# Attention scores of five units as one product per window for both heads, issued two units ahead, without filler products

## Chip, cores and metric

The kernel runs on one core of a Trainium2 chip. The metric is device time of one execution in microseconds; the median of three runs of the kernel before is 808.26 us (806.73 to 808.89).

## What is computed

Windowed attention with eight memory keys per head, then a dense mixture of four experts, then a two-layer network. Cut to what matters:

```python
for c in range(nc):                          # chunks of 32 queries
    k_full = concat(mem_k, k[16 before .. 8 after the chunk])   # 64 keys
    scores = scale * q_c @ k_full.T
    a = exp(scores - max); a = a / (sum(a) + 1e-9)
    out[chunk] = a @ v_full
x = out as (1536 tokens, 512)
x = sum over e of p[:, e] * (relu(x @ w1[e]) @ w2[e])           # 4 experts, 1024 wide
h = x @ w_in
return (max(h, 0) + alpha * min(h, 0)) @ w_out                  # 2048 wide
```

## The kernel before

A **unit** is 128 tokens with all eight heads, four pairs z of two heads e; there are 12 (`NU`), taken in the order of `TURN`. Within a unit four windows of 32 queries see 64 keys each. A unit goes through stages, written as a generator (`unit`): scores on PE into the two PSUM banks of `two`, maximum and subtraction on DVE (`mx`, `pe`), the exponential on ACT (`pe`), four transposes on PE (`t`), a copy on ACT (`pt`), the product with the values on PE (`x`; the 65th column of the values gives the sum), the sums on ACT (`dn`), their reciprocal and the scaling on DVE (`rd`, `xs`), transposes back on PE (`xt`), and the sums, differences and splits into high and low parts (`acc`, `st`, `xh`, `xl`) that the Strassen products of the first layer read. `pe`, `pt` and `xs` are one buffer each, used by all units in turn. Below, scores(2) or x(2) is that stage of the third unit, counted from 0.

Each engine runs its instructions in the order written (`Pinned`). While the first tile of the dense layers has no input, `att_cycle` sets that order: one call starts unit m (scores, maximum, subtraction), then issues x(m-1), exp(m), filler products (`keep_warm`), the transposes of m and those back of m-1. The fillers are products of a zeroed part of `xh` with itself whose result nobody reads: 10 after scores(0), 5 after each of units 1 to 5; from unit 6 on `SOON` puts the first dense products (`a`) there, and `FILL` five more fillers before t(7) and t(8). Once `att["five"]` is 3 the calls end, and the remaining units are woven between the dense products by a planner's clock (`att_poll`).

Scores of a unit are 32 products of 64 rows (the head's dimension), 32 columns and 64 keys, two heads side by side on rows 0 to 63 and 64 to 127. The two ring buffers of `qk` hold two units, `RING_V` half units of values. SP issues all loads in the order written: `load_qk(u + 2)` after scores(u), halves of the values after the x that frees a buffer; the weights of the first layer (`raw`) are four transfers of 128 KB, tied by `begun` to the number of units started.

The dense layers fill the rest of the run: expert layers, conversion of the last weights, the last network.

Of the kernel before, what the change touches and what calls it, by code (L numbers as in the profile page):

```python
# [10 lines left out]
F32 = mybir.dt.float32  # L11
F32R = mybir.dt.float32r
# [38 lines left out]
class Pinned:  # L51


    def __init__(self, tc, eng):
        self.tc, self.eng = tc, eng
# [7 lines left out]
        return call  # L63


@with_exitstack
def tile_kernel(ctx: ExitStack, tc: tile.TileContext, qk, v, wa, wq, dpt, alpha, out):
    nc = tc.nc
    scale = 1.0 / float(D) ** 0.5
    pe_, dve, act, pool, sync = (Pinned(tc, e) for e in (nc.tensor, nc.vector, nc.scalar, nc.gpsimd, nc.sync))  # L70

    cp = ctx.enter_context(tc.tile_pool(name="cp", bufs=1))
    xp = ctx.enter_context(tc.tile_pool(name="xp", bufs=1))
    bp = ctx.enter_context(tc.tile_pool(name="bp", bufs=1))
# [4 lines left out]
    two = scores.enter_context(tc.tile_pool(name="sc", bufs=1, space=bass.MemoryType.PSUM)).tile(  # L79
        [P, 2, 512], F32, tag="two", name="two")  # L80
# [24 lines left out]
    tiny = cp.tile([P, PAD], F32, name="tiny")  # L105
# [9 lines left out]
    now = [0.0]  # L115
# [35 lines left out]


    xh = xp.tile([P, 14, NCOL], F32R, name="xh")
    xl = xp.tile([P, 14, NCOL], F32R, name="xl")

    half = NCOL // 2
    acc = xp.tile([P, KD, 2, 2, half], F32, name="acc")
    acc_all = acc.rearrange("p o t a n -> p o (t a n)")

# [83 lines left out]
    def mm(*a, n, took=None, **kw):  # L243
        pe_.matmul(*a, **kw)
        now[0] += took or 0.013 + n / 2.4e3


    qk_all = bp.tile([P, RING, QW + KW], F32, tag="gg", bufs=2, name="qk")
    qk_t = [qk_all[:, i] for i in range(RING)]
    v_t = [bp.tile([P, V_ROOM], F32, name=f"v{i}", **tag)[:, :VW].rearrange("p (e z w d) -> p e z w d", e=2, z=HP, w=NW)  # L250
           for i, tag in enumerate((dict(tag="w2", bufs=4), dict(tag="w2", bufs=4), dict(tag="fr"), *2 * [dict(tag="v", bufs=2)]))]
    for vt in v_t:
        for e in range(2):
            (pool, dve)[e].memset(vt[:, e], 0.0)
# [5 lines left out]
    def v_of(hu):  # L260
        return v_t[hu % RING_V]

    def load_qk(u, half=slice(0, 2)):
        if u >= NU:
            return
        i = 2 * u % RING
        sync.dma_start(qk_all[:, i + half.start:i + half.stop].rearrange("p h x -> p (h x)"),
                       qk[TURN[u], :, half].rearrange("p h x -> p (h x)"))

    v_next = [0]  # L270

    def load_v(hu):
        assert hu == v_next[0]
        v_next[0] += 1
        if hu >= 2 * NU:
            return
        for e in range(2):
            sync.dma_start(v_of(hu)[e::2, e].rearrange("p z w d -> p (z w d)"), v[TURN[hu // 2], e, :, hu % 2])

    def unit(u):  # L280

# [1 line left out]
        cols = slice(c * BLK, (c + 1) * BLK)  # L283
        win = [slice(w * WIN, (w + 1) * WIN) for w in range(NW)]

        s_ps = two[:, :, :2 * HP * KEYS].rearrange("p e (z k) -> p e z k", k=KEYS)
        now[0] += T_SW
        for half in range(2):
# [9 lines left out]
        load_qk(u + RING // 2)  # L298
        for hu in FIRST_V[u + 1] if u + 1 < len(FIRST_V) else ():
            load_v(hu)  # L300
        mx = cp.tile([P, 2, 2 * HP], F32, tag="mx", bufs=2, name=f"mx{u}")
        dve.tensor_reduce(out=mx, in_=s_ps, axis=AX.X, op=ALU.max)
        dve.tensor_tensor(
            out=pe.rearrange("p z k e -> p e z k"), in0=s_ps,
            in1=mx.unsqueeze(3).to_broadcast([P, 2, 2 * HP, KEYS]), op=ALU.subtract,
        )
        yield LATE
        act.activation(pe, pe, AF.Exp, scale=scale)
        yield LAT[0]
        t_ps = bank(f"t{u}")  # L310
# [11 lines left out]
        for z in range(2 * HP):  # L322
            half, i = divmod(z, HP)
            if z in CUT:
                n = CUT[z]
                parts.append((z, n, bank(f"x{u}_{z}")[:, :2 * n * (D + 1)].rearrange("p (z e d) -> p z e d", e=2, d=D + 1)))
            z0, _, x_ps = parts[-1]
            for w in range(NW):
                mm(x_ps[win[w], z - z0], pt[:, z, win[w]], v_of(2 * u + half)[:, :, i, w], n=2 * (D + 1), took=T_X,
                   start=True, stop=True)  # L330
            if i == HP - 1:
                load_v(2 * u + half + RING_V)
# [65 lines left out]
    def att_poll(force=False):  # L398

        while True:  # L400
            due = [x for x in att["live"] if x[0] <= now[0] and clear(x[2])]
            room = att["next"] < NU and len(att["live"]) < LIVE and clear(att["next"])
            if due:
                x = due[0]
                try:
                    att["stage"][x[2]] += 1
                    lat = next(x[1])
                    x[0] = now[0] + lat
                except StopIteration:
                    att["live"].remove(x)  # L410
                    att["over"].add(x[2])
                    while att["done"] in att["over"]:
                        att["done"] += 1
            elif room and att["start"] <= now[0]:
                g = unit(att["next"])
                att["start"] = now[0] + (PACE0 if force else PACE)
                att["next"] += 1
                x = [0.0, g, att["next"] - 1]
                att["live"].append(x)
                x[0] = next(g) + now[0]  # L420
                att["stage"][x[2]] = 1
            elif force:
                times = [x[0] for x in att["live"] if clear(x[2])]
                if room:
                    times.append(att["start"])
                now[0] = max(now[0], min(times))
                continue
            else:
                return
            if force:  # L430
                return

    def att_cycle():

        m, t0 = att["next"], now[0]
# [23 lines left out]
        x = live[m] = [now[0], unit(m), m]  # L459
        att["live"].append(x)  # L460
        att["next"] += 1
        advance(x)
# [16 lines left out]
    part = {}  # L479
# [626 lines left out]
LATE = 1.6  # L1106
# [100 lines left out]
```

## Time and profile before

| | us |
|---|---|
| median of three runs | 808.26 |
| the profiled execution, its own time | 807.49 |
| span in its trace | 805.7 |
| PE busy | 795.4 (99%) |
| DVE, ACT, POOL busy | 577.4, 324.9, 573.1 |
| PE's share of the chain that ended last | 92% |

The profiled execution is 0.77 us below the median. A timeline row gives start, length, engine, operation, written tile <- read tiles, count, and in brackets the idle time before it with what ended it. Two rows of one engine may overlap by about 0.1 us, since the next starts while the last one drains. A product in float32 appears as two records.

### The profile page before, as it was taken

To read this page: it belongs to the slowest core of one execution; us is meant where nothing else is said; L and a number is where in the kernel's file an instruction comes from. 1 tells how busy PE (TensorE), PEld (TensorE's weight loads), DVE (VectorE), ACT (ScalarE), POOL (GpSimd) and SP (SyncE) were. 2 spreads that over 40 slices of the span, in tenths; PEclk is the share of its full clock that TensorE was granted. 3 is DMA by queue.
4 is the path that set the end of the run, shared out by engine and by line. 5 is a ranking of instruction groups with operands and counts; after the bars stand their busy time and mean duration, and the time that the engine had idled before them with its cause. 6 is when DMAs were issued, how large, how long until landed. Compare 5 with 4: busy or idle time off the path is not lost.

```text
span 805.7 us, 13680 instructions
## 1 busy us (share of the span) xinstructions
PE 795.4 (99%) x5127; PEld 722.9 (90%) x5127; DVE 577.4 (72%) x1009; ACT 324.9 (40%) x726; POOL 573.1 (71%) x598
## 2 busy tenths in 40 slices
PE   9899999999999999999999999999999999999997
PEld 7689989989989989889889899999899988998996
DVE  4676367687687777777777778589975777676554
ACT  4667423224224134133133133145452664565441
POOL 3786768687797696696696793297764878978621
PEclk9999999999999999999999999999999999999999
DMA  8981121231331341321332312001002122221004
GB/s 255 312 281 32 53 67 52 104 132 40 118 105 40 118 144 40 118 93 51 118 119 66 118 39 92 1 27 53 27 26 92 59 73 92 79 92 67 1 1 156
DMA packets 29730, 71.62 MB, mean 89 GB/s; under 512 B 4448, under 2 KB 10592, under 8 KB 29664
## 3 DMA queue, kind: packets, MB, share of 16 engines
q1 hardware_dynamic: 29664, 70.75, 26.3%
q8 instruction: 40, 0.66, 0.3%
q14 instruction: 26, 0.21, 0.1%
HBM read 59.18 MB, written 11.56 MB: 88 GB/s over the span
## 4 chain that ended last, share of the span: by engine, by line
PE 92%; POOL 2%; DVE 2%; DMA 1%; ACT 1%; issue 1%; SPq 0%; DVEq 0%; POOLq 0%; ACTq 0%
PE y L61 48%; PE d L61 12%; PE c L61 12%; PE a L61 12%; PE b L61 6%; DMA qk<-in_qk 1%; PE two L61 1%; POOL gg L61 1%; PE x L61 1%; POOL xl L61 1%; POOL wl L61 1%; PE t L61 1%; PE wps0.0_88 L61 0%; DVE pe L61 0%; DVE mx L61 0%
## 5 line engine op out<-in xcount | busy, mean ns | idle before, releaser
L61 POOL TENSOR_TENSOR gg<-g,gg 128x384 fp32r<-128x384 f32 x192 | 207.2, 1091 | 111.7 <-ACT gg L61 111.1
L61 PE MATMUL y<-gg,wh 128*128 128x512 f32 (+1 forms) x816 | 244.6, 377 | 0.3 <-POOL gg L61 0.3
L61 DVE TENSOR_TENSOR acc<-y,acc 128x512 f32<-128x512 f32 (+1 forms) x244 | 162.5, 677 | 69.7 <-PE y L61 69.6
L61 PEld LDWEIGHTS y<-gg,wh 128*128 128x128 f32 x816 | 151.8, 188 | 24.8 <-POOL gg L61 0.6
L61 PE MATMUL y<-gg,wl 128*128 128x512 f32 (+1 forms) x408 | 153.8, 377 | 0.0
L61 ACT CAST gg<-g 128x384 fp32r<-128x384 f32 x192 | 95.9, 512 | 122.1 <-DVE g L61 120.4
L61 POOL TENSOR_TENSOR wl<-raw,wh 128x256 fp32r<-128x256 f32 (+1 forms) x110 | 112.1, 1024 | 29.4 <-ACT wh L61 27.4
L61 PE MATMUL y<-wh,gg 128*128 128x512 f32 x384 | 120.6, 390 | 0.0
L61 POOL TENSOR_TENSOR wl<-s,wh 128x256 fp32r<-128x256 f32 x88 | 67.2, 767 | 33.4 <-ACT wh L61 33.2
L61 PEld LDWEIGHTS y<-gg,wl 128*128 128x128 f32 x408 | 76.6, 188 | 12.1 <-issue 0.2
L61 PEld LDWEIGHTS y<-wh,gg 128*128 128x128 f32 x384 | 72.1, 188 | 14.7
L61 ACT COPY u<-a 128x384 f32<-128x384 f32 x48 | 23.1, 481 | 151.3 <-PE a L61 150.2
L61 PE MATMUL y<-wl,gg 128*128 128x512 f32 x192 | 74.9, 390 | 0.0
L61 PE MATMUL a<-xh,wh 128*128 128x384 f32 x184 | 62.0, 337 | 0.0
L61 PE MATMUL a<-xh,wl 128*128 128x384 f32 x184 | 61.8, 336 | 0.0
L61 PE MATMUL d<-xh,wh 128*128 128x384 f32 x184 | 61.8, 336 | 0.0
L61 PE MATMUL a<-xl,wh 128*128 128x384 f32 x184 | 61.6, 335 | 0.0
L61 PE MATMUL d<-xh,wl 128*128 128x384 f32 x184 | 61.6, 335 | 0.0
L61 PE MATMUL d<-xl,wh 128*128 128x384 f32 x184 | 61.6, 335 | 0.0
L61 DVE TENSOR_TENSOR u<-b,u 128x384 f32<-128x384 f32 x48 | 26.7, 556 | 48.2 <-PE b L61 47.9
L61 PE MATMUL c<-xl,wh 128*128 128x384 f32 x176 | 58.9, 335 | 0.0
L61 PE MATMUL c<-xh,wh 128*128 128x384 f32 x176 | 58.8, 334 | 0.0
(129 smaller groups left out, 1562.0 us busy)
## 6 DMA issues: line engine op xcount, KB each, us to landing
fr<-in_wq SPq DMA_DIRECT2D x32, 512.0 KB, 3.9
raw<-in_wa SPq DMA_DIRECT2D x28, 512.0 KB, 3.8
w2s<-fl SPq DMA_DIRECT2D x32, 256.0 KB, 2.4
raw<-w2s SPq DMA_DIRECT2D x16, 512.0 KB, 3.5
qk<-in_qk SPq DMA_DIRECT2D x11, 624.0 KB, 5.6
v<-in_v SPq DMA_DIRECT2D x48, 130.0 KB, 4.8
out<-acc SPq DMA_DIRECT2D x12, 256.0 KB, 2.4
pb<-p_dram SPq DMA_DIRECT2D x6, 384.0 KB, 3.7
```

What stands on the lines that cost most here:

```text
L61: return self.tc.keep_in_program_order(f(*a, **kw))
```

## The change

For units 1 to 5 (`WIDE_U` = 6) the keys of a pair of heads stand in a block diagonal: the rows of one head hold its keys, the other half is zero (`clear_k`). One product of 128 rows, 32 columns and 128 keys then gives the scores of both heads: 16 products a unit for 32. Such a unit's scores use one bank of `two`, units in turn (`u % 2`). `att_cycle` for these units issues scores(m+2) in call m, after x(m), and `keep_warm` is called for unit 0 alone. The subtraction moves from the scores' stage to the exponential's. The values of units 1, 2, 4 and 5 come in whole units (`WHOLE`), into `both_v` and a part of `acc` that is not yet written; q and keys of these units are two inputs of their own (`qa`, `ka`), in three slots. `xl` becomes two halves, of which the second first holds the block-diagonal keys. The tables `NEXT_QK`, `FIRST_V`, `NEXT_V` say which loads follow which unit. The bytes loaded for a unit stay 624 KB and 520 KB.

```diff
+    xl = Halves(half, lambda t: xp.tile([P, 14, half], F32R, tag=f"xl{t}", name=f"xl{t}"))
+    both_k = xp.tile([P, 14 * half], F32, tag="xl1", name="both_k")
+    both_v = bp.tile([P, 2, 4, NW * (D + 1)], F32, tag="gg", bufs=2, name="both_v")
...
+    def clear_k(u, engines):
+        for e in range(2):
+            engines[e].memset(wide_k(u)[e * D:(e + 1) * D, 1 - e], 0.0)
...
+        if both(u):
+            sync.dma_start(wide_q(u), qa[u - 1])
+            for e in range(2):
+                sync.dma_start(wide_k(u)[e * D:(e + 1) * D, e], ka[u - 1, e * D:(e + 1) * D])
+            return
...
+            s_ps = two[:, u % 2].rearrange("p (z e k) -> p e z k", e=2, k=KEYS)
...
+        for z in range(2 * HP if both(u) else 0):
+            for w in range(NW):
+                mm(s_ps[win[w], :, z], qv[:, z, win[w]], kv[:, z // HP, z % HP, :, w * STEP:w * STEP + KEYS],
+                   n=2 * KEYS, took=T_X, start=True, stop=True)
+        for half in range(0 if both(u) else 2):
...
         dve.tensor_reduce(out=mx, in_=s_ps, axis=AX.X, op=ALU.max)
+        if both(u):
+            yield LATE
         dve.tensor_tensor(
...
-        yield LATE
+        if not both(u):
+            yield LATE
...
+        att["turn"] += 1
+        if m < WIDE_U:
+            if m == 0:
+                begin_unit(0)
+                at(0, 1)
+                keep_warm(0)
+            at(m, 2)
+            if m == 0:
+                begin_unit(1)
+            at(m + 1, 1)
+            at(m - 1, 4)
+            rest()
+            if m < WIDE_U - 1:
+                at(m, 3)
+            if m + 2 < WIDE_U:
+                begin_unit(m + 2)
...
+WIDE_U = 6
+WHOLE = {1: 0, 2: 1, 4: 0, 5: 1}
+NEXT_QK = {0: (3,), 1: (4,), 2: (5,), 3: (6,), 5: (7,)}
+FIRST_V = {0: ((2, None),), 1: ((3, 0), (3, 1))}
+NEXT_V = {1: ((4, None),), 2: ((5, None),), 3: ((6, 0), (6, 1)), 4: ((7, 0), (7, 1)), 5: ((8, 0),)}
```

PE at the end of the wide units, in the order of the kernel before, from the last of x(4) (the digit in a name is the unit; `two` are scores, here of unit 6):

```order
L61 MATMUL x4_3_628<-v4_118,pt_129 32x130 x4
L61 MATMUL keep5_651<-xh_109 128x384 x5
L61 MATMUL t5_657<-ident_76,pe_131 128x128 x4
L61 MATMUL xt4_663<-ident_76,xs_130 128x128 x4
L61 MATMUL two_75<-qk_113 32x64 x32
L61 MATMUL x5_0_712<-v0_114,pt_129 32x130 x8
L61 MATMUL x5_0_712<-v1_115,pt_129 32x130 x4
L61 MATMUL x5_3_727<-v1_115,pt_129 32x130 x4
```

And of the change, from t(4):

```order
L61 MATMUL t4_507<-ident_76,pe_142 128x128 x4
L61 MATMUL xt3_515<-ident_76,xs_141 128x128 x4
L61 MATMUL x4_0_526<-both_v_111,pt_140 32x130 x12
L61 MATMUL x4_3_539<-both_v_111,pt_140 32x130 x4
L61 MATMUL t5_562<-ident_76,pe_142 128x128 x4
L61 MATMUL xt4_568<-ident_76,xs_141 128x128 x4
L61 MATMUL two_75<-qk_112 32x64 x32
L61 MATMUL x5_0_625<-acc_113,pt_140 32x130 x12
L61 MATMUL x5_3_638<-acc_113,pt_140 32x130 x4
```

The fillers (`keep5`) that stood ahead of t(5) are gone, and scores(5), which stood behind t(4), now stand ahead of it, so that PE has no scores between x(4) and xt(4).

ACT in the same place before, from the copy of t(4) (`pe <- pe` is the exponential, here of unit 5):

```order
L61 COPY pt_129<-t4_561 128x512
L61 COPY acc_111<-xt3_567 128x4x128
L61 CAST xh_109<-st2_474 128x4x128
L61 CAST xh_109<-acc_111 128x4x128
L61 ACTIVATE dn4_635<-x4_0_613,tiny_83 128x6
L61 ACTIVATE dn4_635<-x4_3_628,tiny_83 128x2
L61 ACTIVATE pe_131<-pe_131 128x512
```

And of the change:

```order
L61 COPY pt_140<-t4_507 128x512
L61 ACTIVATE pe_142<-pe_142 128x512
L61 COPY acc_113<-xt3_515 128x4x128
L61 CAST xh_109<-st2_444 128x4x128
L61 CAST xh_109<-acc_113 128x4x128
L61 ACTIVATE dn4_548<-x4_0_526,tiny_83 128x6
L61 ACTIVATE dn4_548<-x4_3_539,tiny_83 128x2
```

The exponential of unit 5 moves from behind the sums of unit 4 (`dn4`) to ahead of them, and with it the copy of xt(3) and two casts stand between the two.

SP before, from its first transfer to the first weights of the dense layers (`raw0`):

```order
L61 DMA qk_113<-in_qk 128x624 x2
L61 DMA qk_113<-in_qk 128x1248
L61 DMA v0_114<-in_v 64x520 x2
L61 DMA v1_115<-in_v 64x520 x2
L61 DMA qk_113<-in_qk 128x1248
L61 DMA v2_116<-in_v 64x520 x2
L61 DMA v3_117<-in_v 64x520 x2
L61 DMA raw0_0_181<-in_wa 128x256 x2
```

And of the change, from the second half of the values of unit 0, which has the same two q-and-key loads ahead of it (`in_qa`, `in_ka` are queries and keys; `both_v` and `acc` take the values of units 1 and 2):

```order
L61 DMA v1_115<-in_v 64x520 x2
L61 DMA qk_112<-in_qa 128x512
L61 DMA both_k_110<-in_ka 64x736 x2
L61 DMA both_v_111<-in_v 64x1040 x2
L61 DMA qk_112<-in_qa 128x512
L61 DMA both_k_110<-in_ka 64x736 x2
L61 DMA acc_113<-in_v 64x4x260 x2
L61 DMA both_k_110<-in_qa 128x512
L61 DMA both_k_110<-in_ka 64x736 x2
L61 DMA v2_116<-in_v 64x520 x2
L61 DMA v3_117<-in_v 64x520 x2
L61 DMA raw0_0_243<-in_wa 128x256 x2
```

The two weight transfers move from behind q and keys of three units and values of two to behind q and keys of five units and values of four. On ACT the two casts that read them stand where they stood, ahead of the sums of unit 2.

## Rows read from the trace of the kernel before

**Rows 1.** The profile's page: busy time of each engine, and TensorE's granted clock.

```profile
PE 795.4 (99%) x5127; PEld 722.9 (90%) x5127; DVE 577.4 (72%) x1009; ACT 324.9 (40%) x726; POOL 573.1 (71%) x598
...
PEclk9999999999999999999999999999999999999999
```

**Rows 2.** Busy time by stretch: us, then busy us per engine, clock, DMA share, GB/s.

```profile
8.40:47.10 38.70, 35.50 (x889) 28.64 (x889) 22.90 (x54) 25.75 (x63) 22.60 (x29) 1.00 0.93 296
47.10:70.00 22.90, 22.09 (x414) 19.51 (x414) 15.31 (x37) 15.95 (x39) 18.57 (x18) 1.00 0.59 188
70.00:805.70 735.70, 730.60 (x3735) 669.35 (x3733) 535.13 (x910) 281.12 (x623) 527.61 (x540) 1.00 0.22 73
```

**Rows 3.** PE in order of time: start us, us, what, idle before it and its releaser.

```profile
13.06 1.07 PE L61 MATMUL two<-qk 64*32 64x64 f32 x64
14.07 1.09 PE L61 MATMUL x<-v,pt 128*32 128x130 f32 x32
15.09 1.16 PE L61 MATMUL keep<-xh 128*128 128x384 f32 x5
16.49 0.66 PE L61 MATMUL t<-ident,pe 128*128 128x128 f32 x4 [0.24 <-ACT pe L61]
16.98 0.60 PE L61 MATMUL xt<-ident,xs 128*128 128x128 f32 x4
17.51 0.96 PE L61 MATMUL two<-qk 64*32 64x64 f32 x64
18.40 1.09 PE L61 MATMUL x<-v,pt 128*32 128x130 f32 x32
...
22.36 0.74 PE L61 MATMUL two<-qk 64*32 64x64 f32 x51 [0.48 <-DMA qk<-in_qk]
...
23.95 1.09 PE L61 MATMUL x<-v,pt 128*32 128x130 f32 x32
...
32.24 0.86 PE L61 MATMUL x<-v,pt 128*32 128x130 f32 x21
```

**Rows 4.** DVE in order of time, one lap of the attention stage.

```profile
14.28 0.69 DVE L61 TENSOR_REDUCE mx<-two 128x8 f32<-128x512 f32 x1 [1.99 <-PE two L61]
15.08 0.69 DVE L61 TENSOR_TENSOR pe<-two,mx 128x512 f32<-128x512 f32 x1
15.69 0.19 DVE L61 RECIPROCAL rd<-dn 128x8 f32<-128x8 f32 x1
15.98 0.76 DVE L61 TENSOR_TENSOR xs<-x,rd 128x384 f32<-128x384 f32 x2
```

**Rows 5.** ACT in order of time, the same lap and the next casts.

```profile
15.01 0.48 ACT L61 ACTIVATE dn<-x,tiny 128x6 f32<-128x6 f32 x2 [1.14 <-PE x L61]
15.80 0.63 ACT L61 ACTIVATE pe<-pe 128x512 f32<-128x512 f32 x1 [0.31 <-DVE pe L61]
16.34 0.60 ACT L61 CAST xh<-acc 128x512 fp32r<-128x512 f32 x1
...
17.66 0.59 ACT L61 COPY acc<-xt 128x512 f32<-128x512 f32 x1
18.14 0.72 ACT L61 CAST wh<-raw 128x256 fp32r<-128x256 f32 x2
```

**Rows 6.** DMA issues from 9 to 10 us: count, KB each, us from issue to landing.

```profile
raw<-in_wa SPq DMA_DIRECT2D x2, 128.0 KB, 5.0
```

**Rows 7.** PE in order of time, around the first dense products.

```profile
42.74 1.09 PE L61 MATMUL x<-v,pt 128*32 128x130 f32 x32
43.76 1.15 PE L61 MATMUL t<-xh 128*128 128x384 f32 x5
...
47.15 1.09 PE L61 MATMUL x<-v,pt 128*32 128x130 f32 x32
```

**Rows 8.** DVE: the first instruction that reads the gate's weights.

```profile
48.41 0.55 DVE L61 SCALAR_TENSOR_TENSOR g<-a,pb 128x384 f32<-128x384 f32 x1
```

**Rows 9.** SP's queue: the transfers of those weights.

```profile
41.84 1.06 SPq L700 DMA_DIRECT2D pb<-p_dram  x2
```

More of the change, by code (lines that the diff above doesn't have):

```diff
@@ L63, in __getattr__, with __init__, __getitem__, tile_kernel @@
         return call
+class Halves:
+    def __init__(self, n, part):
+        self.n, self.part, self.parts = n, part, {}
+    def __getitem__(self, at):
+        rows, chunk, cols = at
+        t = cols.start // self.n
+        if t not in self.parts:
+            self.parts[t] = self.part(t)
+        return self.parts[t][rows, chunk, cols.start - t * self.n:cols.stop - t * self.n]
 @with_exitstack
-def tile_kernel(ctx: ExitStack, tc: tile.TileContext, qk, v, wa, wq, dpt, alpha, out):
+def tile_kernel(ctx: ExitStack, tc: tile.TileContext, qa, ka, qk, v, wa, wq, dpt, alpha, out):
     nc = tc.nc
@@ L153, in tile_kernel @@
     xh = xp.tile([P, 14, NCOL], F32R, name="xh")
-    xl = xp.tile([P, 14, NCOL], F32R, name="xl")
     half = NCOL // 2
+    xl = Halves(half, lambda t: xp.tile([P, 14, half], F32R, tag=f"xl{t}", name=f"xl{t}"))
+    both_k = xp.tile([P, 14 * half], F32, tag="xl1", name="both_k")
+    both_v = bp.tile([P, 2, 4, NW * (D + 1)], F32, tag="gg", bufs=2, name="both_v")
+    qk_all = bp.tile([P, RING, QW + KW], F32, tag="gg", bufs=2, name="qk")
     acc = xp.tile([P, KD, 2, 2, half], F32, name="acc")
@@ L165, in tile_kernel, with both, wide_k, wide_q @@
     spare = slice(NCOL // 2, NCOL)
-    nc.gpsimd.memset(xh[:, 10:14, spare].bitcast(F32), 0.0)
+    def both(u):
+        return 0 < u < WIDE_U
+    def wide_k(u):
+        s = u % 3
+        return both_k[:, 4 * s * KW:4 * (s + 1) * KW].rearrange("p (e h x) -> p e h x", e=2, h=2)
+    def wide_q(u):
+        return both_k[:, 12 * KW:12 * KW + DM] if u % 3 == 1 else qk_all[:, 2 + (u == 3), :DM]
+    def wide_v(u):
+        return acc[:, :, 1, :, :NW * (D + 1)].rearrange("p z e x -> p e z x") if WHOLE[u] else both_v
+    def clear_k(u, engines):
+        for e in range(2):
+            engines[e].memset(wide_k(u)[e * D:(e + 1) * D, 1 - e], 0.0)
     def keep_warm(u):
@@ L245, in mm @@
         now[0] += took or 0.013 + n / 2.4e3
-    qk_all = bp.tile([P, RING, QW + KW], F32, tag="gg", bufs=2, name="qk")
     qk_t = [qk_all[:, i] for i in range(RING)]
@@ L251, in tile_kernel, with clear_v @@
            for i, tag in enumerate((dict(tag="w2", bufs=4), dict(tag="w2", bufs=4), dict(tag="fr"), *2 * [dict(tag="v", bufs=2)]))]
-    for vt in v_t:
+    def clear_v(i, engines):
         for e in range(2):
-            (pool, dve)[e].memset(vt[:, e], 0.0)
+            engines[e].memset(v_t[i][:, e], 0.0)
+    for i in range(2):
+        clear_v(i, (pool, dve))
+    for e in range(2):
+        (pool, dve)[e].memset(both_v[:, e], 0.0)
+    pool.memset(xh[:, 10:14, spare].bitcast(F32), 0.0)
+    clear_k(1, (pool, dve))
+    pool.memset(wide_v(2)[:, 0], 0.0)
+    act.copy(wide_v(2)[:, 1], tiny[:, 2:3].unsqueeze(2).to_broadcast([P, 4, NW * (D + 1)]))
+    clear_v(2, (pool, pool))
+    clear_k(2, (pool, pool))
+    for i in range(3, RING_V):
+        clear_v(i, (pool, pool))
+    clear_k(3, (pool, pool))
     pt, xs, pe = (bp.tile([P, 2 * HP * BLK], F32, tag="ft", bufs=3, name=x) for x in ("pt", "xs", "pe"))
@@ L258, in tile_kernel, with v_of @@
     pe = pe.rearrange("p (z k e) -> p z k e", e=2, k=KEYS)
-    def v_of(hu):
-        return v_t[hu % RING_V]
+    def v_of(u, z, w):
+        if u in WHOLE:
+            return wide_v(u)[:, :, z, w * (D + 1):(w + 1) * (D + 1)]
+        return v_t[V_AT[u, z // HP] % RING_V][:, :, z % HP, w]
     def load_qk(u, half=slice(0, 2)):
@@ L265, in load_qk, with load_v @@
             return
+        if both(u):
+            sync.dma_start(wide_q(u), qa[u - 1])
+            for e in range(2):
+                sync.dma_start(wide_k(u)[e * D:(e + 1) * D, e], ka[u - 1, e * D:(e + 1) * D])
+            return
         i = 2 * u % RING
         sync.dma_start(qk_all[:, i + half.start:i + half.stop].rearrange("p h x -> p (h x)"),
-                       qk[TURN[u], :, half].rearrange("p h x -> p (h x)"))
+                       qk[max(0, u - WIDE_U + 1), :, half].rearrange("p h x -> p (h x)"))
     v_next = [0]
[L272 to L278, printed above, removed]
+    def load_v(*at):
+        for u, h in at:
+            if u >= NU:
+                continue
+            if h is None:
+                for e in range(2):
+                    sync.dma_start(wide_v(u)[e::2, e], v[TURN[u], e].rearrange("k h (z x) -> k (h z) x", z=HP))
+                continue
+            assert V_AT[u, h] == v_next[0], (u, h)
+            v_next[0] += 1
+            for e in range(2):
+                sync.dma_start(v_t[V_AT[u, h] % RING_V][e::2, e].rearrange("p z w d -> p (z w d)"), v[TURN[u], e, :, h])
     def unit(u):
@@ L284, in unit @@
         win = [slice(w * WIN, (w + 1) * WIN) for w in range(NW)]
-        s_ps = two[:, :, :2 * HP * KEYS].rearrange("p e (z k) -> p e z k", k=KEYS)
-        now[0] += T_SW
-        for half in range(2):
+        if both(u):
+            s_ps = two[:, u % 2].rearrange("p (z e k) -> p e z k", e=2, k=KEYS)
+            qv = wide_q(u).rearrange("p (z q) -> p z q", q=BLK)
+            kv = wide_k(u).rearrange("p e h (z k) -> p h z e k", k=SPAN)
+        else:
+            s_ps = two[:, :, :2 * HP * KEYS].rearrange("p e (z k) -> p e z k", k=KEYS)
+        now[0] += T_SW
+        for z in range(2 * HP if both(u) else 0):
[3 more added lines that the diff above has]
+        for half in range(0 if both(u) else 2):
             qk_ = qk_t[(2 * u + half) % RING]
@@ L297, in unit @@
                            n=KEYS, took=T_S, start=True, stop=True)
-        load_qk(u + RING // 2)
-        for hu in FIRST_V[u + 1] if u + 1 < len(FIRST_V) else ():
-            load_v(hu)
+        for x in NEXT_QK.get(u, (u + RING // 2,) if u >= WIDE_U else ()):
+            load_qk(x)
+        load_v(*FIRST_V.get(u, ()))
         mx = cp.tile([P, 2, 2 * HP], F32, tag="mx", bufs=2, name=f"mx{u}")
         dve.tensor_reduce(out=mx, in_=s_ps, axis=AX.X, op=ALU.max)
+        if both(u):
+            yield LATE
         dve.tensor_tensor(
@@ L328, in unit @@
             for w in range(NW):
[L329 to L332, printed above, removed]
+                mm(x_ps[win[w], z - z0], pt[:, z, win[w]], v_of(u, z, w), n=2 * (D + 1), took=T_X, start=True, stop=True)
+            if i == HP - 1 and u >= WIDE_U:
+                load_v(divmod(2 * u + half + RING_V, 2))
+        load_v(*NEXT_V.get(u, ()))
         dn = cp.tile([P, 2 * HP, 2, 1], F32, tag="dn", bufs=2, name=f"dn{u}")
@@ L388, in unit @@
         att["x"] = c + 1
-    att = {"next": 0, "start": 0.0, "done": 0, "over": set(), "live": [], "x": 0, "five": 0, "top": 0, "stage": [0] * (NU + 1)}
+    att = {"next": 0, "turn": 0, "start": 0.0, "done": 0, "over": set(), "live": [], "x": 0, "five": 0, "top": 0, "stage": [0] * (NU + 1)}
     NEED = {0: 3, 2: 4, 3: 5}
@@ L417, in att_poll @@
                 att["next"] += 1
+                att["turn"] = att["next"]
                 x = [0.0, g, att["next"] - 1]
@@ L433, in att_cycle @@
     def att_cycle():
-        m, t0 = att["next"], now[0]
+        m, t0 = att["turn"], now[0]
         live = {x[2]: x for x in att["live"]}
@@ L457, in rest, with begin_unit @@
             begin()
[L459 to L462, printed above, removed]
+        def begin_unit(u):
+            x = live[u] = [now[0], unit(u), u]
+            att["live"].append(x)
+            att["next"] += 1
+            advance(x)
+        att["turn"] += 1
[14 more added lines that the diff above has]
+                begin_unit(m + 2)
+            now[0] = max(now[0], t0 + PACE0)
+            rest()
+            for x in att["live"]:
+                if att["stage"][x[2]] < 5:
+                    x[0] = now[0]
+            return
+        begin_unit(m)
         at(m - 1, 3)
@@ L1024, in tile_kernel @@
     load_qk(1)
-    for hu in FIRST_V[0]:
-        load_v(hu)
+    load_v((0, 0), (0, 1))
+    load_qk(2)
+    load_v((1, None))
     stream("w", weights())
@@ L1052, in begin @@
     def begin():
-        while begun and att["next"] >= begun[0][0]:
+        while begun and att["turn"] >= begun[0][0]:
             begun.pop(0)[1]()
@@ L1130 @@
 RING_V = 5
-FIRST_V = ((0, 1), (2, 3), (4,))
+WIDE_U = 6
[3 more added lines that the diff above has]
+NEXT_V = {1: ((4, None),), 2: ((5, None),), 3: ((6, 0), (6, 1)), 4: ((7, 0), (7, 1)), 5: ((8, 0),)}
+V_AT = {x: i for i, x in enumerate((u, h) for u in range(NU) if u not in WHOLE for h in range(2))}
 WARM = 18
@@ L1188 @@
     probs = inp["moe_domain_probs"].reshape(NU // 2, 2, BLK, E)
+    wide = list(TURN[1:WIDE_U])
     arrays = {
-        "qk": qk,
+        "qa": np.ascontiguousarray(qk[wide][:, :, :, :QW]).reshape(len(wide), P, 2 * QW),
+        "ka": np.ascontiguousarray(qk[wide][:, :, :, QW:]),
+        "qk": np.ascontiguousarray(qk[[TURN[0], *TURN[WIDE_U:]]]),
         "v": np.ascontiguousarray(vs).reshape(NU, 2, KEYS, 2, HP * NW * (D + 1)),
```

## Prediction

> **What bounds the kernel now.** I read the page first: PE is busy 99% of the span and its granted clock stands at 2.4 GHz (9 in each slice) throughout [rows 1]. Next the busy time by stretch, which places the edit. From 70 us to the end PE idles 5.1 us of 735.7. From 47.1 to 70 it idles 0.8 us, and from 8.4 to 47.1, the attention stage, 3.2 us [rows 2]. So behind 47 us nothing waits that could take up a delay: what the attention stage loses or gains reaches the end almost whole. In that stage the DMA engines are busy 93% and move 296 GB/s [rows 2], so transfers set a pace too.
>
> Then PE in order of time. One lap of the stage, x(1) to x(2), takes 18.40 - 14.07 = 4.33 us: x 1.02, fillers 1.16, a wait for exp of 0.24, t 0.49, xt 0.53, scores 0.89 (starts to starts) [rows 3]. Scores(4) waited 0.48 us for their keys, and x(3) came 5.55 us after x(2) [rows 3]. A unit is 624 + 520 KB, 1.17 MB; at 296 GB/s that is 3.96 us, just under the lap. The fillers thus stand in time that PE would otherwise spend waiting.
>
> **The change, part by part.**
>
> Fillers. Five calls of five go, 1.16 us each with about 0.1 of it overlapping the next [rows 3]: 5 x 1.07 = 5.4 us of PE work less.
>
> Scores. The trace has no product of 128 rows, 32 columns and 128 keys, but x has that shape with 130 columns: 32 records in 1.02 us from start to start, against 1.01 and 0.89 for the old scores of 64 records [rows 3]. So a unit's scores cost between nothing and 0.13 us more; I take 0.1, 0.5 us for five. [...]
>
> PE work is therefore 4.9 us less. What counts is whether idle time grows by as much.
>
> The new lap. Scores two units ahead no longer stand in the chain, but DVE and ACT keep their order, and that closes a loop. DVE runs xs(u-1), maximum(u+1), subtraction(u+1), rd(u), xs(u); ACT runs exp(u+1), the copy of xt(u-1), dn(u). Along it: maximum to subtraction 0.80, subtraction to exp 0.72, exp 0.54, copy 0.48, dn to rd 0.68, rd to xs 0.29, xs 0.76 [rows 4, 5]: 4.27 us. A handover inside one engine may overlap by 0.1, so 3.9 at the least. The lap was 4.33. So x(1) and x(2) start where they did, near 14.1 and 18.4, with PE idle instead of running fillers: PE's own share of a lap is 1.02 + 1.02 + 0.49 + 0.53 = 3.1 us.
>
> First weights. Before, they were issued at 9 to 10 us and landed 5.0 us later [rows 6], and ACT's casts at 18.14 did not wait [rows 5]. Now 5 x 624 + 4 x 520 + 256 = 5456 KB, 5.59 MB, must pass before both are in. Data flow from about 2 us (my estimate: the same sum for before gives 3.24 MB / 0.296 + 2 = 13.0, 1.6 us short of 9.6 + 5.0), so they land at 2 + 18.9 = 20.9, or up to 22.5 with that shortfall; I take 21.5. ACT would be at these casts at about 19. dn(2) stands behind them, so it starts at 21.9 (half of 0.72 for the last cast), and xs(2), xt(2) follow: 0.68 + 0.29 + 0.76 + 0.53 puts x(3) at 24.2. Before it was 23.95 [rows 3], then because of keys. No loss against before, but what the fillers freed is spent here, with PE idle for near 3 us. Queued behind on ACT are the casts of xh and the copy of t(3); nothing else needs these.
>
> End of the wide units. x(4) follows one lap later, 28.1 to 28.5. Then PE has only t(5), xt(4) and scores(6). exp(5) starts about 1 us after x(4) does, or 1.9 if the two differences and the reciprocal of the gate that stand ahead of it on DVE cost 0.9 there (estimate). Behind it on ACT stand the copy of xt(3) and two casts: 0.54 + 0.48 + 2 x 0.5 [rows 5]. Then dn to xs 1.73, xt 0.53, scores(6) 0.89: 6.2 to 7.1 us from x(4) to x(5), 5.8 with overlaps. That is 33.9 to 35.6; I take 34.5, against 32.24 before [rows 3]: 2.3 us late.
>
> From x(5) to the dense products. x(7), scores(8), t(8), xt(7) and five fillers move from ahead of the six `b` products to behind them, 43.76 to 47.15 us before [rows 7] holding most of it; the sum of work stays. The second `b` product reads `xl` of unit 5, last made by POOL; I add 0.5 (0 to 1.1). The first use of the gate's weights came at 48.41, with its transfers issued at 41.84 [rows 8, 9]. They are tied to units started, x(6) must free buffers ahead of them in SP's queue, and `b` is now done a unit earlier: they may land behind it, with rd(7) queued behind on DVE. 0 to 1 us, I take 0.2.
>
> The zeroing of block-diagonal keys and of `both_v` is added on POOL (ACT and DVE take a part) between its first memsets and its first `xl`, which follows xt(0); POOL has no other work there, so I put it at nothing. If it ran late, keys of unit 3 would wait. Transfers of whole values carry the same bytes: at nothing.
>
> Sum: 2.3 + 0.5 + 0.2 = **3.0 us slower**. The profiled execution took 807.49, so 810.5; the median lies 0.77 above it, 808.26, so 811.3.
>
> **The rivals.**
>
> *Faster.* If maximum and subtraction slip into DVE's free time and the loop does not bind, transfers do, 3.96 us a unit. For it: DMA is at 93% and buffers are now three units deep. Against: the order of the two engines is fixed. The bound is 4.9 us of work with no new idle; the late weights and the end of the wide units keep some, so 3.3 us faster, 805.0. It decides if x(5) starts before 31 us.
>
> *The clock falls.* This ends far on the slower side. The rows show 2.4 GHz everywhere, with PE busy 35.5 of 38.7 us [rows 2]; my schedule leaves about 27 there (35.5 less 4.9, and less some 4 that move behind `b`), with gaps of 2 to 3 us around 21 and 31. No row shows 1.2 GHz, so I bound a lap there between nothing and a doubling of its 3.1 us; the idle 1.2 of a lap takes the first part, leaving 1.9. Two to four such laps: 4 to 8 us on top of the forecast, 817 in the middle. [...]
>
> *No change.* Weights land near 20.5 and the end of the wide units costs 5 us rather than 6.3: then the loss is about 0.5, 808.8.
>
> **How the numbers follow.** About 0.3% (2.4 us) can be told from no change. The forecast has 0.45, its own range 809 to 814, a third of it under 0.3%. Clock 0.20, no change 0.18, faster 0.17. Slower: 0.30 + 0.20 = 0.50. Same: 0.15 + 0.18 = 0.33. Faster 0.17. The range reaches to the middle of the faster rival, 805.0, and of the clock's, 817.5; that leaves out about 0.18.
>
> **What would show it.** In the trace after: no `keep` rows behind the first ten; scores at about 1.0 us; x(1), x(2) at 14 and 18.4; ACT idle ahead of the first `wh` cast, ended by the transfer `raw`, and PE idle 2 to 3 us ahead of xt(2); x(5) near 34.5; PE idle between 8.4 and 47 us at some 11 us (3.2 + 4.9 + 3.0); clock 9 in all slices. x(5) before 32, or a lap under 3.7 us, would refute the loop; a clock under full speed between 18 and 36 us, or loss behind 70 us, would refute the accounting.

## The result and the profile after

The changed kernel takes **813.37 us** (median; 812.19 to 813.78) against 808.23 for the kernel before in the same comparison: ratio 1.0062, 95% interval 1.0049 to 1.0075, slower by about 5.1 us. The prediction was 811.3, range 805.0 to 817.5. The profiled execution has a span of 811.4 us for 805.7.

Busy time by stretch, columns as in [rows 2]:

```profile
8.40:47.10 38.70, 28.61 (x591) 23.35 (x590) 21.08 (x48) 22.57 (x57) 24.58 (x33) 0.91 0.95 275
47.10:70.00 22.90, 22.07 (x469) 18.80 (x470) 15.63 (x35) 14.05 (x33) 16.08 (x16) 1.00 0.70 217
70.00:811.40 741.40, 736.15 (x3794) 674.17 (x3791) 538.38 (x916) 285.51 (x634) 532.02 (x544) 1.00 0.22 73
```

Behind 70 us PE idles 5.25 us, as before (5.1). So the loss lies ahead of it: from 8.4 to 70 PE idles 10.9 us for 4.0 before. PE's busy time over the three rows falls by only 1.4 us (788.2 to 786.8), where 4.9 of work went; the first row shows why, a granted clock of 0.91. The DMA engines are as busy as before (0.95 for 0.93) and move less (275 for 296 GB/s).

PE in order of time; `two` are scores, here of units 2 to 5, and `x` the products with the values of units 2 to 5:

```profile
13.12 1.08 PE L61 MATMUL two<-both_k,qk 128*32 128x128 f32 x32 [2.43 <-DMA both_k<-in_ka]
...
17.79 1.08 PE L61 MATMUL two<-both_k,qk 128*32 128x128 f32 x32 [1.17 <-DVE rd L61]
...
20.13 1.09 PE L61 MATMUL x<-acc,pt 128*32 128x130 f32 x32 [0.24 <-ACT pt L61]
21.78 1.08 PE L61 MATMUL two<-both_k 128*32 128x128 f32 x32 [0.55 <-DMA both_k<-in_ka]
22.79 0.66 PE L61 MATMUL t<-ident,pe 128*128 128x128 f32 x4
25.19 0.66 PE L61 MATMUL xt<-ident,xs 128*128 128x128 f32 x4 [1.75 <-DVE xs L61]
25.77 1.93 PE L61 MATMUL x<-v,pt 128*32 128x130 f32 x32
27.45 1.95 PE L61 MATMUL two<-both_k,qk 128*32 128x128 f32 x32
...
30.67 1.09 PE L61 MATMUL x<-both_v,pt 128*32 128x130 f32 x32 [0.24 <-ACT pt L61]
...
34.93 0.66 PE L61 MATMUL xt<-ident,xs 128*128 128x128 f32 x4 [2.07 <-DVE xs L61]
...
36.42 1.96 PE L61 MATMUL x<-acc,pt 128*32 128x130 f32 x32
```

Scores(2), (3) and (4) wait 2.43, 1.17 and 0.55 us. The rows of the first and last name the keys' transfer. The row of the second names `rd`, which scores(3) neither read nor overwrite; the keys of unit 3 landed at 17.59, 0.2 us before scores(3) start, so this wait is put down to them as well. The other two waits are those foretold: 1.75 ahead of xt(2), 2.07 ahead of xt(4). x(5) starts at 36.42, 4.2 us later than before [rows 3]. x(3), scores(5) and x(5) take 1.9 us where their like takes 1.1.

ACT in order of time, the casts of the first weights [rows 5] and dn(2) behind them:

```profile
23.06 0.85 ACT L61 CAST wh<-raw 128x256 fp32r<-128x256 f32 x2 [1.51 <-DMA raw<-in_wa]
23.82 0.41 ACT L61 ACTIVATE dn<-x,tiny 128x6 f32<-128x6 f32 x2
```

DVE, the first use of the gate's weights [rows 8], now with a wait for their transfer:

```profile
49.60 0.56 DVE L61 SCALAR_TENSOR_TENSOR g<-a,pb 128x384 f32<-128x384 f32 x1 [0.87 <-DMA pb<-p_dram]
```

The changed kernel's busy time in four stretches of 4 us, columns as above (the clock is the third number from the end):

```profile
20.00:24.00 4.00, 2.76 (x68) 2.08 (x68) 0.41 (x1) 2.08 (x7) 0.46 (x1) 1.00 0.74 226
24.00:28.00 4.00, 2.81 (x48) 2.64 (x52) 2.57 (x6) 2.47 (x9) 2.15 (x7) 0.73 0.96 206
32.00:36.00 4.00, 1.73 (x57) 1.32 (x60) 1.05 (x4) 3.65 (x11) 3.70 (x5) 1.00 0.98 322
36.00:40.00 4.00, 4.00 (x69) 3.30 (x63) 3.62 (x9) 2.72 (x8) 3.71 (x5) 0.57 0.88 191
```

Twice the granted clock stood at 0.50, from 25.9 to 29.2 us and from 36.2 to 39.4 (hence the rows with 0.73 and 0.57), each time about a microsecond behind the end of one of the two long waits (25.19 and 34.93). Products of 384 columns then started 0.32 us apart (38.80, 39.12, 39.44), 1.2 columns per ns, and 0.17 us apart at 1.00 (43.25, 43.42, 43.59). The prediction and the expectations write 1.2 GHz for this state and 2.4, twice as much, for the full clock; the rows give shares of it alone. Three possible causes of the loss stand side by side: late transfers, waits in ACT's and DVE's order, and the clock.

### The profile page after: what moved, and what is told of

Same layout as the page of the kernel before. It is cut to its first block, busy times and chain, and to the rows that moved or that the text cites. A ratio compares the mean times of both kernels' runs of the same rounds, so it can differ in the third digit from the quotient of the medians.

```text
span 811.4 us, 13329 instructions
## 1 busy us (share of the span) xinstructions
PE 794.0 (98%) x4942; PEld 721.7 (89%) x4942; DVE 579.3 (71%) x1008; ACT 325.2 (40%) x727; POOL 580.4 (72%) x608
## 4 chain that ended last, share of the span: by engine, by line
PE 88%; DVE 3%; POOL 3%; DMA 3%; ACT 1%; issue 1%; SPq 0%; DVEq 0%; POOLq 0%; ACTq 0%
PE y L61 46%; PE d L61 11%; PE a L61 11%; PE c L61 11%; PE b L61 6%; PE x L61 1%; POOL xl L61 1%; DMA both_k<-in_qa 1%; POOL gg L61 1%; DMA both_k<-in_ka 1%; DVE acc L61 1%; PE two L61 1%; POOL wl L61 1%; DMA pb<-p_dram 1%; DVE g L61 0%
```

## The experiments

Each was timed against the kernel before in the same comparison. The kernel before had a median of 808.31 beside runs 1 to 4, 808.10 beside runs 5 to 8, 808.41 beside runs 9 to 11 and 808.37 beside run 12, so between these groups the ratios compare better than the medians.

**1. Fillers alone.** The kernel before without `keep_warm` for units 1 to 5; the planner's clock moves on as if they were there.

```diff
-        keep_warm(m)
+        if m == 0 or m >= min(SOON):
+            keep_warm(m)
+        else:
+            now[0] += 0.1 + 5 * (0.013 + NCOL / 2 / 2.4e3)
```

> The kernel before with the fillers of units 1 to 5 left out and nothing else moved: the order of every other instruction is that of before. Theory A (fillers stand in waiting time, and PE's granted clock is what they buy): PE waits about 1.1 us more in each lap, the clock falls below 1.00 somewhere between 14 and 36 us, and the products at 1.2 GHz make it slower, 809.5 to 812. Theory B (the gaps of this order are too short for that; the clock fell in the changed kernel only because its gaps are longer, 1.75 and 2.07 us): clock 1.00 throughout, 808.2 within 0.8. Rival C (fillers cost time today): 803 to 807.

Measured 808.18 us, ratio 1.0001 (0.9990 to 1.0012). By stretch:

```profile
8.40:47.10 38.70, 30.06 (x857) 24.14 (x848) 23.40 (x56) 25.65 (x64) 23.15 (x29) 1.00 0.89 285
47.10:70.00 22.90, 21.10 (x400) 18.34 (x390) 14.29 (x34) 14.93 (x37) 17.27 (x18) 1.00 0.64 207
```

In the first row PE does 5.4 us of work less than in [rows 2], and the time is the same: that work stood in waiting time. The granted clock stayed at 1.00 with waits of up to 1.25 us a lap (ahead of t). Time and clock are those of theory B; its reason, that the clock fell in the changed kernel only because the gaps are longer, is not shown (run 7).

**2. Fillers back in the changed kernel.**

```diff
             if m == 0:
                 begin_unit(1)
+            else:
+                t = now[0]
+                keep_warm(m)
+                now[0] = t
```

> The changed kernel with five fillers put back behind t(m) for units 1 to 5, every other order kept. Theory A (the clock is a cost of its own): the clock is 1.00 in all windows, the slow products of the changed kernel (x(3), scores(5), x(5), first dense products; about 3 us of PE time over their length at full clock) go back to full speed, and the time is 810 to 811.5. Theory B (late keys, late weights and the end of the wide units set the times of x(3) and x(5), the clock only fills waiting time): clock 1.00, but x(5) still starts after 35.5 us and the time is 812.5 to 814.5.

Measured 813.13 us, ratio 1.0060 (1.0048 to 1.0072). The clock was 1.00 in every stretch, x(3) and scores(5) took 1.1 us again, and x(5) came 1.4 us earlier. PE, x(5), and then DVE, the first use of the gate's weights:

```profile
34.99 1.09 PE L61 MATMUL x<-acc,pt 128*32 128x130 f32 x32
```

```profile
49.11 0.56 DVE L61 SCALAR_TENSOR_TENSOR g<-a,pb 128x384 f32<-128x384 f32 x1 [2.01 <-DMA pb<-p_dram]
```

DVE now waits 2.01 us for those weights, against 0.87 in the changed kernel: what the clock gave back was waited out. The time is theory B's, though x(5) came earlier than it said.

**3. First weights' casts behind dn(2).**

```diff
-PREP0 = 11.0
+PREP0 = 14.5
```

> The changed kernel with ACT's two casts of the first weights moved from ahead of dn(2) to behind the copy of xt(2); POOL's two subtractions move with them. Theory (these casts, which wait 1.5 us for their transfer, hold dn(2), and with it xs(2), xt(2) and x(3)): dn(2) at 21.3, xt(2) near 23.4 for 25.19, x(3) near 24.2 for 25.77; if nothing else holds what follows, 811 to 812. Rival (the keys of unit 5, which landed at 26.23, hold scores(5) and the lap behind it): x(3) comes as early, but scores(5) starts at 26.3 or later for 27.45, and the time gains at most 1.1 us: 812.3 to 813.4. If it gains over 3 us, the clock's first fall hung on the gap ahead of xt(2).

Measured 814.77 us, ratio 1.0081 (1.0067 to 1.0096), slower than both said. PE:

```profile
24.10 1.09 PE L61 MATMUL x<-v,pt 128*32 128x130 f32 x32 [0.24 <-ACT pt L61]
27.16 1.08 PE L61 MATMUL two<-both_k,qk 128*32 128x128 f32 x32 [1.96 <-DVE xs L61]
...
47.76 0.45 PE L61 MATMUL b<-xl,wh 128*128 128x384 f32 x1 [2.88 <-POOL xl L61]
```

x(3) came at 24.10, as the theory said, and scores(5) at 27.16, as the rival said (the row names `xs`, which scores(5) do not read; in the packet records the last row of unit 5's keys ended at 26.35). The loss is on a queue that neither priced: POOL's two subtractions moved too, ahead of the low parts `xl`, and the second `b` product waited 2.88 us for those (0.92 in the changed kernel).

**4. Rows of the keys spread.** The block diagonal stays, its rows are dealt to the two heads in turn (queries to match); the zeroing, over all rows now, is moved forward.

```diff
-                sync.dma_start(wide_k(u)[e * D:(e + 1) * D, e], ka[u - 1, e * D:(e + 1) * D])
+                sync.dma_start(wide_k(u)[e::2, e], ka[u - 1, e * D:(e + 1) * D])
...
-            engines[e].memset(wide_k(u)[e * D:(e + 1) * D, 1 - e], 0.0)
+            engines[e].memset(wide_k(u)[:, e], 0.0)
```

> The changed kernel with the block-diagonal keys in another order of rows: the heads of a pair take rows in turn, so that a key transfer writes every second of 128 partitions and not 64 adjoining ones; queries are laid out to match, the zeros are set over all rows of a slot ahead of its first transfer (two memsets of DVE and POOL earlier). Theory (half of the partitions at a time makes the rows of the key transfers slow, 175 ns for 2944 bytes where rows of values of 2080 bytes took 85 before): their rows take 110 to 135 ns, scores(2) start near 11.8 for 13.12, the first weights land near 21.8 for 23.5, and the time is 810.5 to 812. Rival (the transfers are slow because of their number and size, whatever rows they write): 160 ns or more, scores(2) after 12.6, 813 to 814.

Measured 811.52 us, ratio 1.0041 (1.0029 to 1.0053). DMA issues from 5 to 20 us (count, KB each, us from issue to landing), the changed kernel and this run:

```profile
both_k<-in_ka SPq DMA_DIRECT2D x6, 184.0 KB, 6.9
v<-in_v SPq DMA_DIRECT2D x6, 130.0 KB, 4.7
both_v<-in_v SPq DMA_DIRECT2D x2, 260.0 KB, 6.5
```

```profile
both_k<-in_ka SPq DMA_DIRECT2D x7, 184.0 KB, 4.3
v<-in_v SPq DMA_DIRECT2D x6, 130.0 KB, 4.4
...
both_v<-in_v SPq DMA_DIRECT2D x2, 260.0 KB, 4.9
```

Keys land 2.6 us sooner, whole values 1.6. In the packet records of the first 26 us a row of keys (2944 bytes) takes 116 ns at the median for 175; rows of values, which the edit does not touch, gain too (2080 bytes 85 ns for 109, 1040 bytes 47 for 64). The same bytes moved in as many transfers, so which partitions a transfer writes was the cause; why they matter is not shown. The zeroing, which the edit moves as well, does not explain it: the keys of unit 2 were issued at 6.6 us in both runs, and in the changed kernel their zeros were set by 8.4 us, 4.6 before those keys landed. Transfers into 64 adjoining partitions thus took 175 ns a row for 116, and slowed others in flight beside them. PE, scores(2) and x(1), x(2):

```profile
11.57 1.08 PE L61 MATMUL two<-both_k,qk 128*32 128x128 f32 x32 [0.73 <-DVE pe L61]
...
14.03 1.09 PE L61 MATMUL x<-both_v,pt 128*32 128x130 f32 x32
...
18.03 1.09 PE L61 MATMUL x<-acc,pt 128*32 128x130 f32 x32
```

The theory holds, with 1.7 us by the ratios and 1.9 by the medians. A single start says less than the time of a row: scores(2) start from 11.8 to 13.1 us in the three traces with adjoining rows (changed kernel, runs 2 and 3) and from 11.5 to 12.4 in those with spread rows, while a row of keys takes 175 to 187 ns in the former and 116 in all of the latter.

**5. Spread rows and fillers**: the edits of 4 and 2 together.

> The run with the keys' rows spread, with five fillers put back behind t(m) for units 1 to 5. Theory A (with the transfers no longer late, PE's time at 1.2 GHz is on the path): granted clock 1.00, x(5) at 33.8 to 34.5 for 35.32, time 809.5 to 811. Theory B (the fillers take what the clock gives back, or what is gained is waited out behind 44 us, as with fillers alone): 811 to 812.5.

Measured 811.12 us, ratio 1.0038 (1.0025 to 1.0051); the clock was 1.00, and x(5) came at 34.71. The time is theory B's; against run 4 the intervals overlap almost wholly. Against run 2, which differs by the spread rows alone, it is 2.0 us faster by the medians and 1.8 by the ratios: the gain of run 4 again. PE's busy time is that of the kernel before again (788.3), its idle time from 8.4 to 70 us 7.0 for 4.0. So the fall of the clock (0.8 to 0.9 us on each of three products in the changed kernel) costs nothing that fillers don't cost as well.

**6. The gate's inputs earlier**, on top of run 4.

```diff
     load_v((1, None))
+    sync.dma_start(praw, dpt.rearrange("e (p i) -> p e i", i=NI))
...
-        (2, lambda: sync.dma_start(praw, dpt.rearrange("e (p i) -> p e i", i=NI))),
```

> The run with the keys' rows spread, with the transfer of the gate's inputs (24 KB) moved from behind the loads of unit 5 to behind the first values of unit 1; every engine's order is kept. Theory (POOL stands still from 23.2 to 26.56 for this transfer, with the low parts of the input queued behind it, so that the second b product waits for the last of them): POOL's sums start near 23.2, its low parts run 1.5 us or more earlier, the wait of the second b product (1.21) goes, and the time is 810.2 to 811. Rival (POOL waits next for the second pair of first weights, which landed at 26.84 to 27.15, and is then full to 48 us all the same): the wait stays above 0.8, 811 to 812.

Measured 812.29 us, ratio 1.0049 (1.0035 to 1.0063): no gain. The second `b` product still waited 0.91, and the first weights, one transfer further back, landed at 22.48 for 21.82. The theory falls.

**7. First weights ahead of the values of unit 3**, on top of run 6.

```diff
         *[(x, lambda: load_raw(0, 0, 4)) for x in (1, 1)],
+        (1, lambda: load_v((3, 0), (3, 1))),
...
-FIRST_V = {0: ((2, None),), 1: ((3, 0), (3, 1))}
+FIRST_V = {0: ((2, None),)}
```

> As the run before it, and the first two weight transfers stand ahead of the values of unit 3 instead of behind them. Theory (they hold dn(2) on ACT): they land by 20.2 for 21.82, ACT's casts wait 0.3 or less for 1.21, xt(2) starts at 22.0 to 22.5 for 23.52, the clock does not fall between 20 and 28 us, x(3) at 22.6 to 23.2 for 24.57, and the time is 1 to 2 us under that of the run before it, 808.5 to 810. Rival (keys of unit 5 and the values hold the lap behind it): x(3) as early, but x(4) or x(5) gain under 0.5 us and the time is within 0.6 of the run before it.

Measured 810.99 us, ratio 1.0039 (1.0022 to 1.0055). By the medians that is 1.3 under run 6, the gain that the theory named, but by the ratios 0.8, and the intervals overlap; the time is above the 808.5 to 810 of the theory. Nor did its places come: in the profiled execution, whose keys of unit 2 landed 1 us late, the casts still waited 1.30, where the theory had 0.3 or less, and x(3) came at 23.97, where it had 22.6 to 23.2. Against run 4 it is 0.5 by the medians: x(5) came at 33.94 for 35.32, DVE then waited 2.07 for the gate's weights, and hardly anything was left in the end. The clock stayed 1.00, although PE waited longer ahead of xt(4) than the 1.75 us behind which it fell in the changed kernel. PE:

```profile
32.56 0.66 PE L61 MATMUL xt<-ident,xs 128*128 128x128 f32 x4 [1.92 <-DVE xs L61]
```

**8. Casts behind dn(4) as well** (all_moves), on top of run 7.

```diff
-            rest()
+            if m < WIDE_U - 2:
+                rest()
             if m < WIDE_U - 1:
                 at(m, 3)
+            if m > WIDE_U - 3:
+                rest()
```

> As the run before it, and in the last lap of the wide units ACT's two casts behind the copy of xt(3) stand behind dn(4) (some casts and POOL's subtractions behind them move too). Theory (they hold dn(4), the end of the wide units): the wait ahead of xt(4), 2.07, falls to about 1.0, x(5) comes 1.0 earlier than in the run before it, and the time falls by 0.6 to 1.0 more, 807.7 to 809. Rival (transfers or POOL's low parts set what follows): x(5) comes 1.0 earlier and the time stays within 0.4 of the run before it.

Measured 811.54 us, ratio 1.0037 (1.0023 to 1.0051). x(5) starts at 32.75, 3.7 us earlier than in the changed kernel and 0.5 from the kernel before, and the time does not follow. DVE, the first use of the gate's weights:

```profile
47.88 0.56 DVE L61 SCALAR_TENSOR_TENSOR g<-a,pb 128x384 f32<-128x384 f32 x1 [2.17 <-DMA pb<-p_dram]
```

The rival holds: the wait has moved behind x(5). Not all of the 1.2 us by which x(5) came earlier than in run 7 belong to this edit, since here the casts ahead of dn(2) did not wait.

**9. Fewer bytes**, on top of run 8. The values of units 4 and 5 are not loaded; those units read the values of units 1 and 2 from the same buffers.

```diff
-                for e in range(2):
+                for e in range(2 if u < 3 else 0):
```

> The run all_moves with the values of units 4 and 5 not loaded (4 x 260 KB, 1.06 MB; those units use the values of units 1 and 2, which stand in the same buffers); all instructions of the engines stay. Theory (the transfers up to the gate's weights, 12.95 MB by 47.9 us, set the pace of the stage: 1.06 MB at some 290 GB/s are 3.7 us): x(4) does not wait 1.80 for its values, the gate's weights land 3 to 3.7 us earlier, near 44.5, DVE does not wait 2.17 for them, and the time falls by 1.5 to 3 us, to 808.5 to 810. Rival (the loop through DVE and ACT sets the pace): the waits turn into waits for xs and exp at the same places, x(5) within 0.6 of 32.75, and the time falls by 0.5 at most, 811 or more.

Measured 810.44 us, ratio 1.0028 (1.0018 to 1.0038): 1.1 us under run 8 by the medians, 0.7 by the ratios, with intervals that overlap. The gate's weights landed at 45.08 and 45.92, and DVE's wait was gone. x(4) and x(5):

```profile
26.84 1.09 PE L61 MATMUL x<-both_v,pt 128*32 128x130 f32 x32
...
32.72 1.96 PE L61 MATMUL x<-acc,pt 128*32 128x130 f32 x32 [0.32 <-ACT pt L61]
```

x(4) came 1.4 us earlier than in run 8 and x(5) not at all, 5.88 us behind it. Neither theory holds alone: by these traces transfers set the gate's stage, and the order of ACT and DVE sets the end of the wide units.

**10. The gate's weights earlier in SP's queue** (pb_first), on top of run 8, no byte less.

```diff
-        *[(x, lambda ab=ab: load_pb(0, *FIRST[0], (ab,))) for ab, x in enumerate((8, 8))],
+        *[(x, lambda ab=ab: load_pb(0, *FIRST[0], (ab,))) for ab, x in enumerate((7, 7))],
```

> The run all_moves with the transfers of the gate's weights moved ahead of the queries, keys and values of unit 8 and half the values of unit 7 in SP's queue, no byte less. Theory (DVE waits 2.17 for them, with rd(7) queued behind; xt(7), the d products and x(9) wait for it on PE, 0.97, 0.39 and 0.50): they land near 45.5, those waits go, the time falls by 1 to 1.8 us, 809.7 to 810.5. Rival (the values of unit 7 or the keys of unit 8, now behind them, are late instead): PE waits 0.5 to 1.3 for them between 44 and 50 and the time stays within 0.5 of all_moves.

Measured 810.18 us, ratio 1.0024 (1.0013 to 1.0035). The weights landed at 45.14 and DVE's wait was gone. Against run 8 that is 1.4 us by the medians and 1.1 by the ratios, within the theory's range, though the intervals overlap. By stretch:

```profile
8.40:47.10 38.70, 29.41 (x691) 23.14 (x690) 21.81 (x52) 23.74 (x61) 25.61 (x34) 1.00 0.91 284
47.10:70.00 22.90, 22.27 (x415) 19.33 (x415) 15.04 (x35) 15.48 (x38) 15.81 (x16) 1.00 0.65 210
70.00:807.90 737.90, 732.61 (x3746) 670.92 (x3744) 537.39 (x914) 282.40 (x626) 530.14 (x542) 1.00 0.23 73
```

PE works 3.9 us less than before over the three rows and idles 5.9 more from 8.4 to 70 us.

**11. The fillers of units 7 and 8 out**, on top of run 10.

```diff
-FILL = {7: 5, 8: 5}
+FILL = {}
```

> As pb_first, and without the five fillers ahead of t(7) and the five ahead of t(8). Theory (the changed order does one unit less before the b products, so the fillers ahead of t(8), 1.03 us, now stand where PE has no idle time and no longer cover a wait): the time falls by 0.8 to 1.2 against pb_first, mostly behind 50 us, the clock stays 1.00. Rival (they cover the wait for exp(8)): within 0.4 of pb_first.

Measured 810.18 us, ratio 1.0024 (1.0014 to 1.0033), the same as run 10: the rival's time, not the theory's. Behind a wait of 1.49 us that run 10 has as well (1.48), the clock now falls (0.57 over 44 to 48 us, 1.00 in run 10), which the theory did not expect, and x(7) takes 1.96 us. Whether that alone uses up what the fillers took is not shown. PE:

```profile
44.11 0.44 PE L61 MATMUL b<-xl,wh 128*128 128x384 f32 x1 [1.49 <-POOL xl L61]
...
45.74 1.96 PE L61 MATMUL x<-v,pt 128*32 128x130 f32 x32
```

**12. One low part from POOL to DVE**, on top of run 10.

```diff
-        (dve if c == NBLK - 1 else pool).tensor_tensor(
+        (dve if c in (1, NBLK - 1) else pool).tensor_tensor(
```

> As pb_first, and the last low part of unit 4 (1.29 us on POOL at 40.56) is made by DVE, which waits for the b products from 42.1 to 45.2. Theory (POOL, busy without a gap from 31.0 to 46.4, sets the second b product, which waits 1.48): the low parts of unit 5 that it reads start 1.2 earlier, its wait falls to 0.3 to 0.7 (then the cast of ACT that ends at 41.70 sets it), and the time falls by 0.6 to 1.1 against pb_first, 809.1 to 809.6: still above the kernel before. Rival (what is gained there is waited out behind, for the next transfers or the gate's stage): the wait falls, the time stays within 0.4 of pb_first.

Measured 809.74 us, ratio 1.0012 (1.0000 to 1.0024). The wait of the second `b` product fell from 1.48 to 0.75. PE, this product in run 10 and here:

```profile
44.00 0.44 PE L61 MATMUL b<-xl,wh 128*128 128x384 f32 x1 [1.48 <-POOL xl L61]
```

```profile
44.19 0.44 PE L61 MATMUL b<-xl,wh 128*128 128x384 f32 x1 [0.75 <-POOL xl L61]
```

In this execution x(5) started 0.9 us later than in run 10, so the shorter wait did not bring the product forward. By the medians 0.4 us are gained, by the ratios 1.0, with intervals that overlap: inconclusive between theory and rival. It is the fastest version of the change, and its interval does not reach below the kernel before.

## Why the prediction was right, and where not

**Direction and size.** Slower by 3.0 was forecast; 5.1 came. The range, 805.0 to 817.5, took in a faster kernel too, so that it holds says little. The base of the argument holds: the fillers stand in waiting time. Run 1 shows it, 5.4 us of PE work for no time. Place by place the loss was larger than the sum had it: x(5) 4.2 late for 2.3, the second `b` product 0.92 for 0.5, the gate 0.87 for 0.2. These make 6.0, close to the 5.7 by which the two profiled spans differ.

**Scores.** 0.1 a unit was taken. Scores(4) to t(3) is 1.01 us, start to start, against 0.89 for the 64 records of the old ones [rows 3]: 0.12.

**The lap.** 3.9 to 4.3 us through DVE and ACT. Where transfers were in time it was 4.00 (run 4, x(1) to x(2)) and 3.75 (run 9, x(3) to x(4)), a little under the lower end. In the changed kernel it was 4.60, with the keys late.

**The term that was missing** is the new form of the keys' transfers. "Transfers of whole values carry the same bytes: at nothing" is the one sentence on a transfer's form; the keys' form is priced nowhere, and the landing of the first weights was reckoned by bytes alone. The keys went into 64 adjoining partitions: those of unit 2 landed at 12.99, where the kernel before had them at 11.11 and run 4 at 11.14, and transfers behind them were late. Run 4 puts 1.7 to 1.9 us on it, most of the 2.1 by which the forecast fell short.

**First weights.** The mechanism was right (ACT's casts wait, with dn(2), xt(2) and x(3) behind), the landing mis-sized: 23.5 for 21.5, since it was reckoned at 296 GB/s. Run 4 has 21.8. x(3) came at 25.77 for 24.2. But neither attempt at this wait gained much in time: in run 3 POOL's wait took its place, in run 7 part of it stayed and the gate's took over.

**End of the wide units.** x(4) to x(5) took 5.75 us; 6.2 to 7.1 was written, 5.8 with overlaps. It took 5.88 in run 9, which has the casts moved as in run 8 and does not load the values of units 4 and 5: the wait ahead of xt(4) fell from 2.07 to 1.04 there, but the wait ahead of t(5) for exp(5) grew from 0.44 to 1.12, so that the end of the wide units is not shorter.

**The first dense products.** `b` waited 0.92 for `xl` (0.5 taken, 0 to 1.1), DVE 0.87 for the gate's weights (0.2 taken, 0 to 1). The places were right, their weight was not seen: since `b` now comes a unit earlier, these two take back much of what is gained ahead of them. From run 8 to run 12, which relieves both, the ratio falls from 1.0037 to 1.0012, 2.0 us; runs 6 to 8 together, which work ahead of `b`, take it from 1.0041 to 1.0037, 0.3 us.

**The clock.** The rival given 0.20 did happen, behind the two gaps it named (around 21 and 31 us there, ending at 25.2 and 34.9 here). That gaps bring the clock down was the author's estimate, since no row of before shows a fall; run 1, with waits of up to 1.25 us, kept 1.00, and the changed kernel went to 0.50 behind 1.75 and 2.07. The price did not come: 4 to 8 us were put on top (the middle is written as 817 and as 817.5; the sum gives 817.3). No run shows that term: three products took 0.8 to 0.9 us more each, and with the clock back at 1.00 by fillers (runs 2 and 5) the time is the same. "9 in all slices" was wrong. That this did not spoil the forecast is luck: the fall came where a later wait took up what it cost (run 2).

**What stays open.** Run 12 leaves about 1 us (0 to 2), and why the freed work (4.9 us by the forecast, 3.9 by run 10's trace) turns wholly into waiting is shown only in part: the end of the wide units and the wait of the second `b` product (0.75) remain. Fewer wide units were not tried, nor the new order with the old scores, nor the loads of whole values by themselves.

## To carry to other kernels

Work that stands in waiting time is worth nothing when removed (run 1: 5.4 us of it, no time gained); ask first what ends the wait, here the order of two other engines and the transfers. When a load is given a new shape, price it by which partitions it writes as well as by its bytes (run 4: 175 ns a row for 116), and look at the transfers behind it. When a consumer is moved earlier (`b`, the gate), move its inputs in every queue too, or it can give back what the stage ahead of it gained (run 8: x(5) 1.2 us earlier, no gain in time, DVE waiting 2.17 us for the gate's weights).

## What the runs showed that was not expected

Transfers into 64 adjoining partitions slowed those around them: untouched rows of 2080 bytes took 109 ns beside them and 85 without. And the length of a wait did not tell by itself whether the clock came down: behind 1.49 us it fell without fillers (run 11), behind 1.48 with five fillers ahead of t(7) it did not (run 10), and behind 1.92 us in run 7, with no fillers in units 1 to 5, it did not either.
